# A maxout FFN written with differences: from token group 2 on, x*(w1*w_out) plus a maximum against zero

## The chip, the cores and the metric

The kernel runs on one core of one Trainium2 chip. The metric is device microseconds of the whole program. The kernel before was timed three times; the median is 475.64 us.

## The reference

Two blocks follow each other. The first is a gated linear attention (HGRN2 with an outer-product state), for 4 batches, 8 heads, 768 time steps and head dimension 48:

```
f = 1 / (1 + exp(-f_logit))
for t in range(S):
    state = f[t][:, None] * state + outer(k[t], v[t])
    y[t] = q[t] @ state
```

Its output, with the 8 heads side by side, is x with 3072 tokens and 384 features. The second block is a feed-forward network (FFN) with three weights of 384 x 768 and one of 768 x 384:

```
h = maximum(maximum(x @ w1, x @ w2), x @ w3)
out = h @ w_out
```

Everything is computed in float32; the weights arrive as 64-bit numbers.

## The kernel before, in words

**Units and groups.** Attention is cut in 24 units (`NU`). A unit is a chunk of 64 time steps of two batches, with all 8 heads, so 128 tokens. Four units (`GRP`) make a group of 512 tokens (`TOK`), and the FFN works on a group. There are six groups, 0 to 5. (The title counts them from 1: group 2 there is `g == 1` in the code.)

**Attention.** For each unit VectorE (DVE) runs two scans over the gates (lines 316 and 334), VectorE or GpSimd (POOL) multiply k and q with them (lines 327 and 338), and TensorE (PE) makes scores (`pairs`, line 379), which VectorE masks (line 382), then the values part (line 398) and the state update (`sums`, line 419), and at last the part of y that comes from the carried state (`finish`, line 465). From unit 8 on (`BY_ROWS`), k, q and f arrive by rows in eight small transfers for each tensor and pair of units (line 182), and VectorE turns 32x32 blocks (lines 283 and 369); before that PE transposes them. ScalarE (ACT) copies y to `heads` (line 471), and `pack` (line 486) moves it with ten DMAs per call to `xT`, whose partitions are features. For units 0 to 3, PE transposes x instead (line 454). The first three units of a group are packed in its last unit, the fourth in the first unit of the next group, half of these DMAs issued by SyncE (SP), half by ScalarE.

**FFN.** `ffn(g, xT)` is a generator. For each of 6 blocks of 128 hidden features (`NJ`) and each of the 3 weights it accumulates a product over 3 slices of 128 input features (`NK`) into a PSUM tile `p` of 128 x 512 (line 513). The first product is copied by ScalarE to `top` (line 520), the second and third are joined to it by maxima on VectorE (line 522), the last of which writes `hm`. Then for each of 4 tiles of 128 tokens, 6 matmuls with 384 columns accumulate `hm` times `w_out` (line 538); ScalarE copies the result to `o` (line 543), and SyncE sends it out (line 548). There are two `p` buffers (`ps_f`), and they are also used by everything else in the FFN. In group 0 the first two blocks are done by halves of 256 tokens.

**Weights.** The 64-bit weights come in 24 pieces. Each is rounded to float32 by ScalarE (lines 228 to 232), VectorE (lines 239 to 242) and POOL (line 246), in step with the FFN of group 0: after each product `round_begin` and `round_end` are called for the next pieces. Later the pieces are loaded once more and ScalarE checks their range (lines 257 and 266 to 269).

**The order.** It is written out by hand under `tc.manual_schedule()`: each engine executes its instructions in the order in which the program emits them. FFN work of the last complete group stands between the pieces of attention: `pending` holds generators, and `fill(n)` lets the first one run n steps, where a step ends at each `yield`. A product of 512 columns has two steps (two matmuls, then one), an output tile two of three matmuls each. What is left of a group when the next one is appended is done first. After the last unit, `finish`, `pack` and the FFN of group 5 are left.

Of the kernel before, what the change touches and what calls it, by code (L numbers as in the profile page):

```python
# [46 lines left out]
C = 64  # L47
# [8 lines left out]
def kernel(  # L56
# [27 lines left out]
    make_identity(nc, ident)  # L84
    w_in = [const.tile([128, NK, DFF], FP32, name=f"w_in{i}") for i in range(3)]
    w_out = const.tile([128, NJ, DM], FP32, name="w_out")
    low = const.tile([1, 1], I32, name="low")

    def fast():
        ctx = ExitStack()  # L90
        with ctx:
# [398 lines left out]

            HALF = TOK // 2
            J_HALF = 2

            def ffn(g, xT):
                hm = work.tile([128, NJ, TOK], FP32, name="hm", bufs=1)


                steps = [(j, slice(0, TOK)) for j in range(NJ)]
                if g == 0:
                    steps = [(j, slice(n * HALF, (n + 1) * HALF)) for n in range(2) for j in range(J_HALF)] + steps[J_HALF:]  # L500
                done, n_step = 1, 0
                for j, t in steps:
                    w = t.stop - t.start
                    for i in range(3):
                        p = ps_f.tile([128, TOK], FP32, name="p")[:, 0:w]
                        for kt in range(NK):
                            if g:
                                rhs = xT[:, kt, :]
                            elif w < TOK:
                                rhs = by_halves(xT)[:, t.start // HALF, kt, :]  # L510
                            else:
                                rhs = by_halves(xT)[:, :, kt, :]
                            nc.tensor.matmul(p if g or w < TOK else p.rearrange("p (two t) -> p two t", two=2),  # L513
                                             lhsT=w_in[i][:, kt, j * 128:(j + 1) * 128], rhs=rhs,
                                             start=(kt == 0), stop=(kt == NK - 1))
                            if kt == 1 and w == TOK:
                                yield
                        if i == 0:
                            top = work.tile([128, TOK], FP32, name="top")[:, 0:w]
                            nc.scalar.copy(top, p)  # L520
                        else:
                            nc.vector.tensor_tensor(hm[:, j, t] if i == 2 else top, p, top, op=ALU.max)  # L522

                        if g == 0:
                            n_step += 1
                            ahead = n_step + 1 if n_step <= 6 else 7 + (n_step - 6) * 5 // 6 if n_step <= 12 else 12 + (n_step - 12) * 6 // 5
                            for r in range(done, min(ahead, len(pieces))):
                                if r + 2 < len(pieces):
                                    round_begin(r + 2)
                                if r + 1 < len(pieces):  # L530
                                    round_end(r + 1)
                                done = r + 1
                            load_weights(2, done)
                        yield
                for i in range(GRP):
                    p = ps_f.tile([128, TOK], FP32, name="p")
                    for j in range(NJ):
                        nc.tensor.matmul(p[:, 0:DM], lhsT=hm[:, j, i * UT:(i + 1) * UT], rhs=w_out[:, j, :],  # L538
                                         start=(j == 0), stop=(j == NJ - 1))
                        if j == NJ // 2 - 1:  # L540
                            yield
                    o = work.tile([UT, DM], FP32, name="o", bufs=3)
                    nc.scalar.copy(o, p[:, 0:DM])  # L543
                    c, bp = divmod(g * GRP + i, 2)
                    for a in range(2):
                        t0 = (2 * bp + a) * S + c * C
                        last = g * GRP + i == NU - 1 and a
                        (nc.scalar if last else nc.sync).dma_start(out=out[t0:t0 + C, :], in_=o[a * C:(a + 1) * C, :])  # L548
                    yield

            pending = []

            def fill(n):
                while n and pending:
# [14 lines left out]
                return work.tile([128, NK, TOK], FP32, name="xT")  # L569

            CHECKS = 2 * GRP + 3

            with tc.manual_schedule():
# [56 lines left out]
                fill(1)  # L633
                keys(3)
                sums(2)
                y_by_tokens(2)
                pairs(3)
                fill(1)
                x_of_tokens(2, xT)
                fill(1)  # L640
                values(3)
                fill(1)
                sums(3)
                fill(1)
                y_by_tokens(3)
                load(GRP + 1)
                load_v(GRP + 1)
# [7 lines left out]
                fill(2)  # L655
                for u in range(GRP, NU):
                    n = u + 1
                    fill(0 if u == 2 * GRP else 4 if u % 2 and u > 2 * GRP else 2)
                    keys(u)
                    keys_by_blocks(u, 2)  # L660
                    if u > GRP:
                        finish(u - 1)
                        if u % GRP == 3:
                            pack(0, 2, xT)
                        elif u % GRP == 0:
                            pack(3, 3, xT, both)
                    if u % GRP == 0:
                        if u > GRP:
                            pending.append(ffn(u // GRP - 1, xT))
# [14 lines left out]
                    fill(2)  # L684
# [4 lines left out]
                    fill(2)  # L689
                    if BY_ROWS <= u + 2 < NU and u % GRP == 0:  # L690
                        load(u + 2, one, "k")
                    values(u)
# [1 line left out]
                        carry(n)  # L694
                    if CHECKS <= u < CHECKS + len(pieces) // 2:
                        check_range(2 * (u - CHECKS) + 1)
                    fill(1 if u < 2 * GRP else 2)
                    if CHECKS <= u + 2 < CHECKS + len(pieces) // 2:
                        check_load(2 * (u + 2 - CHECKS))
                        check_load(2 * (u + 2 - CHECKS) + 1)  # L700
                    if BY_ROWS <= u + 2 < NU and u % GRP == 0:
                        load(u + 2, one, "q")
                    keys_by_blocks(n, 0)
                    if u >= 2 * GRP:
                        fill(2)
                    keys_by_blocks(n, 1)
                fill(2)
# [20 lines left out]
    def general():  # L728
        G, AHEAD = 128, 3
# [243 lines left out]
```

## Time and profile before

| what | value |
| --- | --- |
| median of three runs | 475.64 us (473.46 to 476.57) |
| span of the profiled execution (first to last instruction) | 472.3 us; the page gives no other time for it |
| PE busy | 455.4 us, 96% |
| DVE, ACT, POOL busy | 266.4, 146.1, 105.5 us |
| matmul records of the FFN's products (line 513) | 684, 290.3 us |
| matmul records of the FFN's outputs (line 538) | 288, 96.6 us |
| mean granted TensorE clock | 0.999 of full speed |

The page first gives each engine's busy time, its share of the span and its instruction count. In the row of slices that follows, the span is cut in 40 equal parts, and a digit is the busy share in tenths. A float32 matmul leaves two records, so 684 records are 342 matmuls: 306 of 512 columns and 36 of 256. The durations of neighbouring records overlap[...]. "PEld" is the weight load, "SPq" and "ACTq" are issues of DMAs by these engines, and `A <- B` in a view of waits reads "A sat idle until B was done".

### The profile page before, as it was taken

To read this page: it belongs to the slowest core of one execution; us is meant where nothing else is said; L and a number is where in the kernel's file an instruction comes from. 1 tells how busy PE (TensorE), PEld (TensorE's weight loads), DVE (VectorE), ACT (ScalarE), POOL (GpSimd) and SP (SyncE) were. 2 spreads that over 40 slices of the span, in tenths; PEclk is the share of its full clock that TensorE was granted. 3 is DMA by queue.
4 is the path that set the end of the run, shared out by engine and by line. 5 is a ranking of instruction groups with operands and counts; after the bars stand their busy time and mean duration, and the time that the engine had idled before them with its cause. 6 is when DMAs were issued, how large, how long until landed. Compare 5 with 4: busy or idle time off the path is not lost.

```text
span 472.3 us, 10233 instructions
## 1 busy us (share of the span) xinstructions
PE 455.4 (96%) x4068; PEld 247.8 (52%) x4068; DVE 266.4 (56%) x528; ACT 146.1 (31%) x339; POOL 105.5 (22%) x125
## 2 busy tenths in 40 slices
PE   4989999999999999999999999999999999999995
PEld 3767655556445456545456445445544445444453
DVE  6876757687478675497685487585585220021110
ACT  2434757421201325144224144233243211100000
POOL 2153636432033031232130230230321200000000
PEclk9999999999999999999999999999999999999999
DMA  9998997234768043778343577544460012100002
GB/s 135 207 257 235 277 221 91 42 69 78 115 87 192 22 82 102 154 98 148 83 83 107 96 136 93 151 82 114 87 138 1 0 51 49 36 1 1 2 17 53
DMA packets 177141, 47.13 MB, mean 100 GB/s; under 512 B 154816, under 2 KB 175552, under 8 KB 177088
## 3 DMA queue, kind: packets, MB, share of 16 engines
q1 hardware_dynamic: 172528, 45.25, 48.5%
q10 hardware_dynamic: 4560, 1.18, 1.5%
q8 instruction: 33, 0.54, 0.5%
q14 instruction: 20, 0.16, 0.1%
HBM read 37.75 MB, written 4.72 MB: 90 GB/s over the span
## 4 chain that ended last, share of the span: by engine, by line
PE 82%; SPq 5%; DMA 4%; DVE 3%; issue 1%; ACTq 1%; ACT 1%; DVEq 0%
PE p L513 54%; PE p L538 16%; DMA f_ld<-in_f_logit_dram 4%; PE y L465 2%; PE y L398 2%; SPq L182 2%; PE a L379 2%; PE y L419 2%; PE tr L278 1%; ACTq L486 1%; SPq L163 1%; DMA xT<-heads 1%; DVE r L316 1%; SPq L548 1%; PE y L394 1%
## 5 line engine op out<-in xcount | busy, mean ns | idle before, releaser
L513 PE MATMUL p<-xT,w_in 128*128 128x512 f32 (+1 forms) x684 | 290.3, 575 | 1.6 <-POOL w_in L246 0.8
L513 PEld LDWEIGHTS p<-xT,w_in 128*128 128x128 f32 x684 | 126.2, 190 | 134.9 <-issue 124.8
L538 PE MATMUL p<-w_out,hm 128*128 128x384 f32 x288 | 96.6, 490 | 0.6 <-DVE top L522 0.6
L522 DVE TENSOR_TENSOR top<-p,top 128x512 f32<-128x512 f32 (+1 forms) x38 | 25.0, 657 | 102.4 <-PE p L513 101.6
L538 PEld LDWEIGHTS p<-w_out,hm 128*128 128x128 f32 x288 | 53.8, 190 | 38.4 <-issue 1.7
L369 DVE STREAM_TRANSPOSE ks<-kh 32x128 f32<-32x128 f32 x224 | 67.7, 302 | 3.6
L520 ACT COPY top<-p 128x512 f32<-128x512 f32 (+1 forms) x38 | 21.4, 562 | 139.9 <-PE p L513 139.8
L326 POOL COPY ends<-r 128x8 f32<-128x8 f32 x24 | 7.7, 320 | 187.1 <-DVE r L316 187.1
L522 DVE TENSOR_TENSOR hm<-p,top 128x512 f32<-128x512 f32 (+1 forms) x38 | 24.8, 652 | 32.6 <-PE p L513 32.6
L327 POOL TENSOR_TENSOR kh<-kt,r 128x512 f32<-128x512 f32 x16 | 31.4, 1960 | 36.5 <-DVE kt L283 26.1
L543 ACT COPY o<-p 128x384 f32<-128x384 f32 x24 | 11.4, 476 | 89.8 <-PE p L538 85.7
L471 ACT COPY heads<-y 64x256 f32<-64x256 f32 (+1 forms) x60 | 22.1, 369 | 43.1 <-PE y L465 36.5
L316 DVE TENSOR_TENSOR_SCAN r<-gate,from_one 128x520 f32<-128x520 f32 x24 | 29.8, 1240 | 9.2 <-ACT gate L295 5.2
L334 DVE TENSOR_TENSOR_SCAN prod<-gate,from_inv 128x520 f32<-128x520 f32 x24 | 30.2, 1259 | 0.0
L246 POOL TENSOR_TENSOR w_in<-top_bits,rest_bits 128x384 uint32<-128x384 uint32 x18 | 21.1, 1180 | 30.3 <-DVE top_bits L240 12.1
L382 DVE TENSOR_TENSOR at<-a,mask 128x512 f32<-128x512 f32 x24 | 16.5, 689 | 14.4 <-PE a L379 14.0
L283 DVE STREAM_TRANSPOSE gate<-sig 128x512 f32<-128x512 f32 x16 | 11.3, 705 | 16.2 <-ACT sig L298 16.2
L344 POOL TENSOR_TENSOR state<-st,ends 128x384 f32<-128x384 f32 x22 | 19.2, 872 | 0.2
L338 POOL TENSOR_TENSOR qh<-qt,prod 128x512 f32<-128x512 f32 x16 | 18.8, 1176 | 1.5 <-DVE qt L283 1.5
L398 PEld LDWEIGHTS y<-at,v_ld 64*64 64x64 f32 x640 | 11.1, 134 | 14.1 <-issue 9.0
L465 PEld LDWEIGHTS y<-qh,state 48*48 48x48 f32 x640 | 10.3, 119 | 12.3 <-issue 12.3
L379 PE MATMUL a<-qh,kh 48*64 48x64 f32 x768 | 15.7, 219 | 0.5 <-DVE qh L338 0.3
(89 smaller groups left out, 308.8 us busy)
## 6 DMA issues: line engine op xcount, KB each, us to landing
raw<-in_moe_w_dram SPq DMA_DIRECT2D x36, 384.0 KB, 5.1
v_ld<-in_v_dram SPq DMA_DIRECT2D x48, 96.0 KB, 3.2
raw<-in_moe_w_out_dram SPq DMA_DIRECT2D x12, 384.0 KB, 4.8
out_dram<-o SPq DMA_DIRECT2D x47, 96.0 KB, 2.2
xT<-heads SPq DMA_DIRECT2D x30, 72.0 KB, 2.2
f_ld<-in_f_logit_dram SPq DMA_DIRECT2D x32, 64.0 KB, 2.6
k_ld<-in_k_dram SPq DMA_DIRECT2D x32, 64.0 KB, 2.4
q_ld<-in_q_dram SPq DMA_DIRECT2D x32, 64.0 KB, 2.6
```

The costliest lines, as they stand in the source:

```text
L246: nc.gpsimd.tensor_tensor(dst, by(top), by(rest), op=ALU.add)
L316: nc.vector.tensor_tensor_scan(r[:, 0:LEN][:, ::-1], flat(gate)[:, ::-1], flat(from_one)[:, ::-1], 1.0, op0=ALU.mult, op1=ALU.max)
L327: (nc.vector if u < BY_ROWS else nc.gpsimd).tensor_tensor(kh.rearrange("p h a t -> p a h t"), kt, by_batch(r[:, 1:LEN + 1].rearrange("p (x ...
L334: nc.vector.tensor_tensor_scan(flat(prod), flat(gate_tiles[u % 2]), flat(from_inv[u % 2]), 1.0, op0=ALU.mult, op1=ALU.max)
L369: nc.vector.transpose(ks[n * 32:(n + 1) * 32, :, par, e0:e0 + 32], kh[p0:p0 + 32, :, a, t0:t0 + 32])
L379: nc.tensor.matmul(p[t, par, hp * C:(hp + 1) * C], lhsT=kh[r, hp, a, :], rhs=qh[r, a, hp, :], start=True, stop=True)
L398: nc.tensor.matmul(y[o:o + DP, a, hp * C:(hp + 1) * C], lhsT=v_ld[s, 2 * hp + par, :], rhs=d["at"][s, par, hp, :], start=(hp == 0), stop=F ...
L471: nc.scalar.copy(heads[o, :, t0 + a * C:t0 + (a + 1) * C], y[i, a, 0:HP * C].rearrange("p (h t) -> p h t", h=HP))
L513: nc.tensor.matmul(p if g or w < TOK else p.rearrange("p (two t) -> p two t", two=2), lhsT=w_in[i][:, kt, j * 128:(j + 1) * 128], rhs=rhs, ...
L520: nc.scalar.copy(top, p)
L522: nc.vector.tensor_tensor(hm[:, j, t] if i == 2 else top, p, top, op=ALU.max)
L538: nc.tensor.matmul(p[:, 0:DM], lhsT=hm[:, j, i * UT:(i + 1) * UT], rhs=w_out[:, j, :], start=(j == 0), stop=(j == NJ - 1))
```

## The change

With a = x*w1, the maximum of the three products is a + max(0, x*(w2-w1), x*(w3-w1)). So the FFN's output is x*(w1*w_out) + max(0, x*(w2-w1), x*(w3-w1))*w_out. Groups 1 to 5 compute this form; group 0 keeps the old one (`ffn_first`).

Behind the products of group 0 the weights are remade in place, between its four output tiles: `apart` subtracts w1 from w2 and w3 (VectorE), `turn` transposes w1 (PE, copied back by ScalarE), and `linear` multiplies it with `w_out` into `w_lin`, which lies in the place of w1. In groups 1 to 5 a block then has two products: the first is copied through Relu by ScalarE, the second is joined by one maximum on VectorE. An output tile has three matmuls of x with `w_lin` ahead of the six of `hm` with `w_out`, all in one accumulation.

Each `yield` now returns an amount of PE time, and `fill(ns)` adds to a budget and runs steps until it is used up. The amounts in the program change with that: five `fill(PART)` with `PART = 2740` in a unit, the last of them 1000 less in units 4 to 7. The last `pack` of a group is issued by SyncE alone, except for that of the last group. In the last two units ScalarE reads one element of y after the values part (`seen`).

```diff
+    w_lin = w_in[0][:, :, 0:DM]
...
+                if u >= NU - 2:
+                    seen = work.tile([1, 1], FP32, name="seen")
+                    nc.scalar.copy(seen, y[0:1, 1, (HP - 1) * C:(HP - 1) * C + 1])
...
-            def ffn(g, xT):
...
+            COLUMN = 4 / 2.4
+
+
+            def product(g, xT, j, i, t):
+                w = t.stop - t.start
...
+                    if kt == 1 and w == TOK:
+                        yield 2 * w * COLUMN
+                return p
+
...
+            def outputs(g, hm, i, xT=None):
+                p = ps_f.tile([128, TOK], FP32, name="p")
+                if g:
+                    for kt in range(NK):
+                        nc.tensor.matmul(p[:, 0:DM], lhsT=xT[:, kt, i * UT:(i + 1) * UT], rhs=w_lin[:, kt, :],
+                                         start=(kt == 0), stop=False)
+                    yield NK * DM * COLUMN
+                for j in range(NJ):
+                    nc.tensor.matmul(p[:, 0:DM], lhsT=hm[:, j, i * UT:(i + 1) * UT], rhs=w_out[:, j, :],
+                                     start=(g == 0 and j == 0), stop=(j == NJ - 1))
+                    if j == NJ // 2 - 1:
+                        yield NJ // 2 * DM * COLUMN
...
+            def apart(j):
+
+                first = w_in[0][:, :, j * 128:(j + 1) * 128]
+                for w in w_in[1:]:
+                    piece = w[:, :, j * 128:(j + 1) * 128]
+                    nc.vector.tensor_tensor(piece, piece, first, op=ALU.subtract)
+
+            def turn(j):
+
+                p = ps_f.tile([128, TOK], FP32, name="p")
+                piece = w_in[0][:, :, j * 128:(j + 1) * 128]
+                for a in range(NK):
+                    nc.tensor.transpose(p[:, a * 128:(a + 1) * 128], piece[:, a, :], ident)
+                nc.scalar.copy(piece, p[:, 0:DM].rearrange("q (a c) -> q a c", a=NK))
+                yield DM * COLUMN
+
+            def linear(a):
+
+                p = ps_f.tile([128, TOK], FP32, name="p")
+                for j in range(NJ):
+                    nc.tensor.matmul(p[:, 0:DM], lhsT=w_in[0][:, a, j * 128:(j + 1) * 128], rhs=w_out[:, j, :],
+                                     start=(j == 0), stop=(j == NJ - 1))
+                    if j % 2:
+                        if j == NJ - 1:
+                            nc.scalar.copy(w_lin[:, a, :], p[:, 0:DM])
+                        yield 2 * DM * COLUMN
+
+            def ffn_first(xT):
...
+                        yield (1 if w == TOK else NK) * w * COLUMN
                 for i in range(GRP):
+                    for j in range(i * NJ // GRP, (i + 1) * NJ // GRP):
+                        apart(j)
+                    yield from outputs(0, hm, i)
+                    for j in range(i * NJ // GRP, (i + 1) * NJ // GRP):
+                        yield from turn(j)
+                for a in range(NK):
+                    yield from linear(a)
+
+            def ffn(g, xT):
+                hm = new_hm()
+                for j in range(NJ):
+                    for i in (1, 2):
+                        p = yield from product(g, xT, j, i, slice(0, TOK))
+                        if i == 1:
+                            top = new_top(TOK)
+                            nc.scalar.activation(top, p, AF.Relu)
+                        else:
+                            nc.vector.tensor_tensor(hm[:, j, :], p, top, op=ALU.max)
+                        yield TOK * COLUMN
+                for i in range(GRP):
+                    yield from outputs(g, hm, i, xT)
 
+            budget = [0.0]
+
+            def fill(ns):
+                budget[0] += ns
+                while budget[0] > 0 and pending:
                     try:
-                        next(pending[0])
-                        n -= 1
+                        budget[0] -= next(pending[0])
                     except StopIteration:
                         pending.pop(0)
 
                 return work.tile([128, NK, TOK], FP32, name="xT")
 
             CHECKS = 2 * GRP + 3
+            STEP = NK * HALF * COLUMN
+            PART = 2740
...
-                pending.append(ffn(0, xT))
-                fill(1)
+                pending.append(ffn_first(xT))
+                fill(STEP)
...
-                    fill(0 if u == 2 * GRP else 4 if u % 2 and u > 2 * GRP else 2)
+                    fill(PART)
...
-                            pack(3, 3, xT, both)
+                            pack(3, 3, xT)
...
-                    fill(1 if u < 2 * GRP else 2)
+                    fill(PART)
...
-                    if u >= 2 * GRP:
-                        fill(2)
+                    fill(PART - 1000 if u < 2 * GRP else PART)
...
-                fill(12)
+                fill(20000)
...
-                fill(6)
+                fill(9000)
-                fill(99)
+                fill(10 ** 6)
```

`product`, `new_hm` and `new_top` hold what stood in `ffn` before. `ffn_first` has the loop over products with the calls of `round_begin`, `round_end` and `load_weights` as before.

More of the change, by code (lines that the diff above doesn't have):

```diff
@@ L492, in fast @@
             J_HALF = 2
-            def ffn(g, xT):
[L495 to L500, printed above, removed]
+            COLUMN = 4 / 2.4
+            def product(g, xT, j, i, t):
+                w = t.stop - t.start
+                p = ps_f.tile([128, TOK], FP32, name="p")[:, 0:w]
+                for kt in range(NK):
+                    if g:
+                        rhs = xT[:, kt, :]
+                    elif w < TOK:
+                        rhs = by_halves(xT)[:, t.start // HALF, kt, :]
+                    else:
+                        rhs = by_halves(xT)[:, :, kt, :]
+                    nc.tensor.matmul(p if g or w < TOK else p.rearrange("p (two t) -> p two t", two=2),
+                                     lhsT=w_in[i][:, kt, j * 128:(j + 1) * 128], rhs=rhs,
+                                     start=(kt == 0), stop=(kt == NK - 1))
+                    if kt == 1 and w == TOK:
+                        yield 2 * w * COLUMN
+                return p
@@ new lines, in new_hm, with new_top @@
+            def new_hm():
+                return work.tile([128, NJ, TOK], FP32, name="hm", bufs=1)
+            def new_top(w):
+                return work.tile([128, TOK], FP32, name="top")[:, 0:w]
+            def outputs(g, hm, i, xT=None):
+                p = ps_f.tile([128, TOK], FP32, name="p")
+                if g:
+                    for kt in range(NK):
+                        nc.tensor.matmul(p[:, 0:DM], lhsT=xT[:, kt, i * UT:(i + 1) * UT], rhs=w_lin[:, kt, :],
[6 more added lines that the diff above has]
+                        yield NJ // 2 * DM * COLUMN
+                o = work.tile([UT, DM], FP32, name="o", bufs=3)
+                nc.scalar.copy(o, p[:, 0:DM])
+                c, bp = divmod(g * GRP + i, 2)
+                for a in range(2):
+                    t0 = (2 * bp + a) * S + c * C
+                    last = g * GRP + i == NU - 1 and a
+                    (nc.scalar if last else nc.sync).dma_start(out=out[t0:t0 + C, :], in_=o[a * C:(a + 1) * C, :])
+                yield NJ // 2 * DM * COLUMN
@@ L501, in ffn @@
+            def ffn_first(xT):
+                hm = new_hm()
+                steps = [(j, slice(n * HALF, (n + 1) * HALF)) for n in range(2) for j in range(J_HALF)]
+                steps += [(j, slice(0, TOK)) for j in range(J_HALF, NJ)]
                 done, n_step = 1, 0
@@ L504, in ffn @@
                     for i in range(3):
[L505 to L517, printed above, removed]
+                        p = yield from product(0, xT, j, i, t)
                         if i == 0:
-                            top = work.tile([128, TOK], FP32, name="top")[:, 0:w]
+                            top = new_top(w)
                             nc.scalar.copy(top, p)
@@ L522, in ffn @@
                             nc.vector.tensor_tensor(hm[:, j, t] if i == 2 else top, p, top, op=ALU.max)
[L524 to L533, printed above, removed]
@@ L534, in ffn @@
-                        yield
-                for i in range(GRP):
[L536 to L549, printed above, removed]
+                        n_step += 1
@@ new lines, in ffn_first @@
+                        ahead = n_step + 1 if n_step <= 6 else 7 + (n_step - 6) * 5 // 6 if n_step <= 12 else 12 + (n_step - 12) * 6 // 5
+                        for r in range(done, min(ahead, len(pieces))):
+                            if r + 2 < len(pieces):
+                                round_begin(r + 2)
+                            if r + 1 < len(pieces):
+                                round_end(r + 1)
+                            done = r + 1
+                        load_weights(2, done)
@@ new lines, in ffn_first @@
+                        yield (1 if w == TOK else NK) * w * COLUMN
+                for i in range(GRP):
+                    for j in range(i * NJ // GRP, (i + 1) * NJ // GRP):
[6 more added lines that the diff above has]
+            def ffn(g, xT):
+                hm = new_hm()
+                for j in range(NJ):
[4 more added lines that the diff above has]
+                            nc.scalar.activation(top, p, AF.Relu)
+                        else:
+                            nc.vector.tensor_tensor(hm[:, j, :], p, top, op=ALU.max)
+                        yield TOK * COLUMN
+                for i in range(GRP):
+                    yield from outputs(g, hm, i, xT)
@@ L551, in fast @@
             pending = []
-            def fill(n):
-                while n and pending:
-                    try:
-                        next(pending[0])
-                        n -= 1
+            budget = [0.0]
+            def fill(ns):
+                budget[0] += ns
+                while budget[0] > 0 and pending:
+                    try:
+                        budget[0] -= next(pending[0])
                     except StopIteration:
@@ L628, in fast @@
                 round_begin(2)
-                pending.append(ffn(0, xT))
-                fill(1)
+                pending.append(ffn_first(xT))
+                fill(STEP)
                 before(3)
                 values(2)
-                fill(1)
+                fill(STEP)
                 keys(3)
@@ L637, in fast @@
                 pairs(3)
-                fill(1)
+                fill(STEP)
                 x_of_tokens(2, xT)
-                fill(1)
+                fill(STEP)
                 values(3)
-                fill(1)
+                fill(STEP)
                 sums(3)
-                fill(1)
+                fill(STEP)
                 y_by_tokens(3)
@@ L651, in fast @@
                 after(GRP)
-                fill(2)
+                fill(2 * STEP)
                 before(GRP)
                 carry(GRP)
-                fill(2)
+                fill(2 * STEP)
                 for u in range(GRP, NU):
                     n = u + 1
-                    fill(0 if u == 2 * GRP else 4 if u % 2 and u > 2 * GRP else 2)
+                    fill(PART)
                     keys(u)
@@ L683, in fast @@
                         check_range(2 * (u - CHECKS))
-                    fill(2)
+                    fill(PART)
                     keys_by_blocks(u, 3)
@@ L688, in fast @@
                         before(n)
-                    fill(2)
+                    fill(PART)
                     if BY_ROWS <= u + 2 < NU and u % GRP == 0:
@@ L696, in fast @@
                         check_range(2 * (u - CHECKS) + 1)
-                    fill(1 if u < 2 * GRP else 2)
+                    fill(PART)
                     if CHECKS <= u + 2 < CHECKS + len(pieces) // 2:
@@ L703, in fast @@
                     keys_by_blocks(n, 0)
-                    if u >= 2 * GRP:
-                        fill(2)
+                    fill(PART - 1000 if u < 2 * GRP else PART)
                     keys_by_blocks(n, 1)
-                fill(2)
+                fill(PART)
                 finish(NU - 1)
```

## The prediction

> **What bounds the kernel now.** I read the engine totals first, then the slices, then what TensorE (PE) waits for, then the chain that ended last, from which the prices come.
>
> ```profile
> PE 455.4 (96%) x4068; PEld 247.8 (52%) x4068; DVE 266.4 (56%) x528; ACT 146.1 (31%) x339; POOL 105.5 (22%) x125
> PE   4989999999999999999999999999999999999995
> DVE  6876757687478675497685487585585220021110
> PEclk9999999999999999999999999999999999999999
> ```
>
> PE is busy 455.4 of 472.3 us, at full clock, in every slice but the first two and the last; VectorE (DVE) is at 56%. The view of PE's waits says whether anything else decides:
>
> ```profile
> PE tr L278 <- DMA f_ld<-in_f_logit_dram: 6.5, 3, 5.9
> PE p L438 <- DVE st L427: 1.5, 1, 1.5
> PE p L513 <- POOL w_in L246: 0.8, 1, 0.8
> PE p L513 <- DVE hm L522: 0.7, 1, 0.7
> PE p L538 <- DVE top L522: 0.6, 1, 0.6
> ```
>
> The columns are total us, times, longest. All but the first loads sum to some 6 us, all before unit 8. From about 105 us on PE is fed without a gap: the kernel takes as long as PE's work. The reader is to see that only PE work removed, or a new PE wait, can move the end.
>
> The chain of waits at the end is pure FFN, so prices are clean there (start, duration, what):
>
> ```profile
> 405.36 15.45 PE p L513 x36
> 420.98 31.10 PE p L513 x72
> 452.07 15.49 PE p L538 x48
> ```
>
> A float32 matmul leaves two records, so 72 records are 36 matmuls of 512 columns: 31.10/36 = 0.864 us each. 48 records are 24 matmuls of 384 columns: 15.49/24 = 0.645 us. For 128x128 transposes the timeline has two sets of four, back to back:
>
> ```profile
> 57.83 0.60 PE L278 MATMUL tr<-ident,k_ld 128*128 128x128 f32 x4
> 58.26 0.60 PE L278 MATMUL tr<-ident,q_ld 128*128 128x128 f32 x4
> ```
>
> 58.26 - 57.83 = 0.43 us for four, 0.108 us each; transposes are not split in two records.
>
> [...]the 512-column records last 597 ns in the mean, while they follow each other every 432 ns; so I price from chain stretches, not from means. [...]the 128x384 addition of line 427 took 532. [...]the trace has one table load (1.28 us) for sigmoid, sign, abs and relu. [...]here an issue takes about 0.59 us.
>
> **The change, part by part, on PE.**
> - *w1 product gone from groups 1 to 5*: 5 groups x 6 blocks x 3 contraction steps = 90 matmuls of 512 columns, 90 x 0.864 = 77.8 us less. All on the path.
> - *x*(w1*w_out) added in their outputs*: 5 groups x 4 row tiles x 3 = 60 matmuls of 384 columns, 60 x 0.645 = 38.7 us more.
> - *Weight products, once*: 6 x 3 = 18 transposes, 1.9 us; 3 x 6 = 18 matmuls of 384 columns, 11.6 us.
> - Net: -77.8 + 38.7 + 1.9 + 11.6 = -25.6 us. Attention's matmuls and group 0's products stay.
>
> **On the other engines.**
> - *DVE*: [...]30 maxima of 0.684 us leave later (-20.5 us). Behind the subtractions in DVE's queue stand the mask, k and q work of units 7 and 8. The largest batch[...] is followed by 12 small transposes (3.8 us) before unit 8's mask; meanwhile PE has a row tile, three transposes, two linear matmuls and unit 7's state products, some 8 us. I take nothing[...].
> - *ScalarE (ACT)*: nine evictions of the weight stage at 0.48 us, 4.3 us, at 31% load: hidden but for the handover below. Relu replaces a copy of the same shape (584 ns): nothing; at most 0.1 us each were it slower, and a product (2.6 us) covers that. The two `seen` copies wait for PE's y in units 22 and 23; behind them in ACT's queue are FFN evictions. PE has just issued that work, so I take 0, at most 0.5 us each.
> - *Two FFN accumulators*: a turned block is only 3 x 0.108 = 0.33 us of PE, less than the copy (0.48[...]) that frees the other buffer. Four handovers stall (output 1 behind turn 0, output 2 behind turn 2, turn 5, first linear product): about 0.35, 0.35, 0.3, 0.2. I take 1.2 us, 0 to 3.
> - *Weights of group 0*: FFN now gets 12.7 us per unit in units 4 to 7 where it got 7 half-steps, about 9. So it finishes one attention unit earlier; unit work apart from FFN being about 3 us, the last rounded weights are wanted some 3 us sooner. They have room: the last w_in piece is rounded near 77 us and used after 94. Early pieces are tight (the 0.8 us wait), and rounding, maxima and scans share DVE and ACT more densely. I take 1 us, 0 to 3.
> - *Head rows to xT*: a new group's first product needs the transfer of the last unit's heads, and PE needs old FFN work meanwhile. Before, at unit 16:
>
> ```profile
> 249.14 0.67 PE L465 MATMUL y<-qh,state 48*48 48x64 f32 x32
> 249.87 1.14 ACT L471 COPY heads<-y 128x256 f32<-128x256 f32 x3
> 251.04 3.09 ACTq L486 DMA_DIRECT2D xT<-heads  x5
> 256.33 3.60 SPq L486 DMA_DIRECT2D xT<-heads  x5
> 263.19 7.03 PE L513 MATMUL p<-xT,w_in 128*128 128x512 f32 x16
> ```
>
> The last piece is issued near 259.3 and lands near 261.1, 11.3 us after the y products ended; PE turned to the new group at 263.2. The SyncE (SP) half began 5 us after the ACT half, behind a weight reload that waited 5.5 us for ACT's transfers. The change puts all ten issues on SP, so that crossing goes, and ACT's sigmoid, held 3.2 us, comes sooner. New need: heads copies 1.2, nine issues 9 x 0.59 = 5.3, landing 1.9, together 8.4 us, if SP is free. Cover, counted from PE's order: unit 8, 16 linear matmuls, about 12 us; units 12 and 16, 12 output matmuls plus mask and values products (1.6), 9.3; unit 20, nine, 7.4; the end, where both queues still share, nine, 5.8. At the end the need was 6.7 us (y products end 393.55, last issue about 398.3, landing 1.9). Stalls: 1.0 at unit 20, 0.9 at the end, 1.9 together. Bounds: 0, and rival A. Reloads, k and q rows queue behind the ten issues on SP; with the 5 us wait gone they are earlier than before, and q rows, 1.0 us late once, gain room.
>
> Sum: 1.2 + 1.0 + 1.9 = 4.1 us of new waits. Against the profiled execution: 472.3 - 25.6 + 4.1 = 450.8 us of span. The page gives no time of the profiled execution beyond its span; the median, 475.64, lies 3.3 us above it, and I carry that: 450.8 + 3.3 = 454.1, so 454.
>
> The budget itself (a step is charged 1.667 ns a column where the chain shows 0.864/512 = 1.688) changes order, not sum. Turns are charged 0.64 us where they take 0.33: 1.9 us in all of units with less cover.
>
> **Rivals.**
> A. *The heads arrive late.* If SP is held as before and the transfer takes 11.3 us at units 12, 16, 20, with cover 9.3, 9.3, 7.4, PE loses 2.0 + 2.0 + 3.9, and 0.9 at the end: 8.8 instead of 1.9. With the weight stage at its upper ends (3 + 3) that is 472.3 - 25.6 + 14.8 + 3.3 = 464.8. For: no cover was short before, all are shorter now. Against: what held SP was the crossing of queues, which goes. 0.17.
> B. *No stall at all*: 472.3 - 25.6 + 3.3 = 450.0. For: PE was gapless for 360 us. Against: three covers and a handover that come out negative. 0.15.
> C. *Slower: attention's chain becomes the bound.* FFN per unit falls from about 15 to 13.6 us, so a unit shrinks from 18.1 (72.4 us per group) to 16.8 us. If sigmoid, transposes, scans, POOL products and mask of a unit needed over 18.4 us, sixteen units would cost 16 x 1.6 = 26 us, what was saved; at 18.75, 31 us: 472.3 - 25.6 + 31 + 3.3 = 481. It decides from 18.4 us a unit. Against: DVE works 12.3 us a unit (24.65 in 36 us), and unit 17's chain ran from sigmoid at 254.2 to q product at 262.4, 8 us. 0.04.
> D. *It doesn't do what it says* (fewer matmuls gone): PE's order shows 216 products of 512 columns where there were 306, so excluded.
>
> **Numbers.** Forecast 0.64 (451 to 458), A 0.17, B 0.15, C 0.04. The range 450 to 463 takes in B and most of A. Runs of the kernel before spread by 0.65%, so within 1% counts as no change (470.9 to 480.4). Faster by over 1%: forecast, B, and nearly all of A, 0.93; same 0.03; slower 0.04.
>
> **What would show it.** In the page after: 432 PE records of 512 columns (612 before) and 444 of 384 (288 before); PE busy near 430 us and still over 94%; DVE near 250. Waits of PE for "DMA xT<-heads" of about 1 us at unit 20 and the end; waits for ACT copies between 90 and 115 us near 1 us. Wrong if PE waits on xT for several us at each group, on DVE or POOL in every unit, or if 384-column matmuls that switch between x and hm cost more than 0.645 us.

## The result and the profile after

The changed kernel took 457.93 us (median of four runs, 457.55 to 458.81), the kernel before beside it 474.73 (473.46 to 476.57): a ratio of 0.9635, 95% interval 0.9595 to 0.9675. The profiled execution has a span of 456.2 us.

First the engine totals and slices of the changed kernel:

```profile
PE 432.9 (95%) x4062; PEld 244.1 (54%) x4062; DVE 253.4 (56%) x510; ACT 150.1 (33%) x350; POOL 103.9 (23%) x125
PE   4989999999999999999999999999989999999995
DVE  6976757556858569357779557759456520011100
PEclk9999999999999999999999999999999999999999
```

PE's busy time fell from 455.4 to 432.9 us, by 22.5. Its idle time, span less busy, rose from 16.9 to 23.3 us, by 6.4. The difference, 16.1 us, is the fall of the span. The PE row now has an 8 late in the kernel where it had nines only. The groups of instructions, different shapes apart, show what remains of each sort of matmul (records, then total busy us and mean ns):

```profile
L511 PE MATMUL p<-xT,w_in 128*128 128x512 f32 x432 | 195.3, 600 | 6.6 <-ACT top L612 2.8 <-DVE hm L614 1.9 <-DMA xT<-heads 1.8
L532 PE MATMUL p<-w_out,hm 128*128 128x384 f32 x288 | 99.3, 491 | 1.3 <-ACT w_in L558 1.0 <-ACT o L537 0.2
L528 PE MATMUL p<-w_in,xT 128*128 128x384 f32 x120 | 42.4, 489 | 0.0
```

With the 36 records (12.4 us) of the product w1*w_out, there are 432 records of 512 columns and 288 + 120 + 36 = 444 of 384, as forecast. The 512-column group was 272.7 us before, so 77.4 us went. The last column, idle time ahead of the group with its releasers, has grown: before, it was 0.2 us for the 512-column products. The waits of PE after (total us, times, longest) say the same, with the stages around them:

```profile
PE tr L279 <- DMA f_ld<-in_f_logit_dram: 5.1, 1, 5.1
PE p L511 <- ACT top L612: 2.8, 4, 0.7
PE p L511 <- DVE hm L614: 1.9, 3, 0.6
PE p L511 <- DMA xT<-heads: 1.8, 1, 1.8
...
PE p L532 <- ACT w_in L558: 1.0, 1, 1.0
...
PE p L557 <- ACT o L537: 0.3, 1, 0.3
PE p L511 <- POOL w_in L247: 0.3, 1, 0.3
PE p L532 <- ACT o L537: 0.2, 1, 0.2
```

Lines 2 to 4 are 6.5 us. They fall in units 8 to 23, where PE had waited for nothing that counts. From unit 8's scores to unit 23's PE was idle 0.3 us before (105.1 to 377.1 us) and 7.0 us after (119.6 to 375.0). Line 4 is the wait at unit 20. Lines 2 and 3 were not in the forecast: PE wants one of the two FFN accumulators and neither is empty. Unit 17 in the timeline shows how that comes about (start, duration, work, idle time before it in brackets):

```profile
276.43 1.28 DVE L370 STREAM_TRANSPOSE ks<-kh 32x128 f32<-32x128 f32 x4
277.74 0.71 DVE L284 STREAM_TRANSPOSE kt<-k_ld 128x512 f32<-128x512 f32 x1
278.38 1.20 DVE L335 TENSOR_TENSOR_SCAN prod<-gate,from_inv 128x520 f32<-128x520 f32 x1
279.41 1.13 PE L511 MATMUL p<-xT,w_in 128*128 128x512 f32 x2
280.57 0.60 ACT L612 ACTIVATE top<-p 128x512 f32<-128x512 f32 x1 [2.47 <-PE p L511]
280.67 0.71 DVE L284 STREAM_TRANSPOSE qt<-q_ld 128x512 f32<-128x512 f32 x1 [1.09 <-POOL kh L328]
281.22 7.13 PE L511 MATMUL p<-xT,w_in 128*128 128x512 f32 x16 [0.69 <-ACT top L612]
281.31 0.65 DVE L614 TENSOR_TENSOR hm<-p,top 128x512 f32<-128x512 f32 x1
```

The program emits `ks`, `kt`, `prod` and `qt`, VectorE's part of the attention work, between the two steps of a block's second product. PE has nothing of its own at that place and runs the product through, so its row shows no gap. But the maximum that empties this product (`hm`, line 614) is emitted behind the four and runs only at 281.31. The product that ends near 280.5, the next block's first, was in the other accumulator. PE then waits 0.69 us until ScalarE has emptied that one. `qt`, ahead of the maximum, had itself waited 1.09 us; at two of the other three waits of line 2 (ending at 214.82 and 350.24) it had waited 2.73 and 2.98 us, where its two waits before the change were 1.03 and 0.84.

### The profile page after: what moved, and what is told of

It is laid out like the page before. It is cut to its first block, busy times and chain, and to the rows that moved or that the text cites. A ratio compares the mean times of both kernels' runs of the same rounds, so it can differ in the third digit from the quotient of the medians.

```text
span 456.2 us, 10209 instructions
## 1 busy us (share of the span) xinstructions
PE 432.9 (95%) x4062; PEld 244.1 (54%) x4062; DVE 253.4 (56%) x510; ACT 150.1 (33%) x350; POOL 103.9 (23%) x125
## 4 chain that ended last, share of the span: by engine, by line
PE 84%; DVE 5%; ACT 4%; DMA 4%; issue 2%; SPq 1%; POOL 0%; ACTq 0%; DVEq 0%
PE p L511 42%; PE p L532 18%; PE p L528 7%; PE y L470 3%; PE p L565 3%; PE y L399 2%; PE y L424 2%; PE a L380 2%; DVE r L317 2%; DMA raw<-in_moe_w_out_dram 2%; ACT heads L476 1%; PE tr L279 1%; DMA xT<-heads 1%; ACT sig L299 1%; PE y L395 1%
## 5 line engine op out<-in xcount | busy, mean ns | idle before, releaser
L511 PE MATMUL p<-xT,w_in 128*128 128x512 f32 (+1 forms) x504 | 212.8, 569 | 7.5 <-ACT top L612 2.8
L511 PEld LDWEIGHTS p<-xT,w_in 128*128 128x128 f32 x504 | 92.0, 190 | 104.2 <-issue 85.2
L532 PE MATMUL p<-w_out,hm 128*128 128x384 f32 x288 | 99.3, 491 | 1.3 <-ACT w_in L558 1.0
L614 DVE TENSOR_TENSOR hm<-p,top 128x512 f32<-128x512 f32 x30 | 20.4, 681 | 80.9 <-PE p L511 80.5
L327 POOL COPY ends<-r 128x8 f32<-128x8 f32 x24 | 6.7, 279 | 187.0 <-DVE r L317 187.0
L612 ACT ACTIVATE top<-p 128x512 f32<-128x512 f32 x30 | 17.8, 594 | 91.9 <-PE p L511 91.9
L528 PE MATMUL p<-w_in,xT 128*128 128x384 f32 x120 | 42.4, 489 | 0.0
L528 PEld LDWEIGHTS p<-w_in,xT 128*128 128x128 f32 x120 | 22.5, 190 | 16.0 <-issue 1.9
L399 PEld LDWEIGHTS y<-at,v_ld 64*64 64x64 f32 x640 | 11.2, 134 | 13.0 <-issue 6.1
```

What stands on the lines that cost most here:

```text
L528: nc.tensor.matmul(p[:, 0:DM], lhsT=xT[:, kt, i * UT:(i + 1) * UT], rhs=w_lin[:, kt, :], start=(kt == 0), stop=False)
L614: nc.vector.tensor_tensor(hm[:, j, :], p, top, op=ALU.max)
```

## The experiments

Ratios are to the kernel before, run on the same chip beside the kernel; the changed kernel's is 0.9635.

### Is it the order or the arithmetic?

**Order alone.** The arithmetic of the kernel before, three products and two maxima a block, with everything else of the changed kernel: steps given out by the budget (slots of 1772 ns in units 4 to 7, 3124 after), the last `pack` of a group on SyncE alone, and `seen`. This cut of the edit is against the kernel before; those further down are against the changed kernel.

```diff
-            def fill(n):
-                while n and pending:
+            def fill(ns):
+                budget[0] += ns
+                while budget[0] > 0 and pending:
                     try:
-                        next(pending[0])
-                        n -= 1
+                        budget[0] -= next(pending[0])
```

> Old mathematics (three products, two maxima, no weight products), new handing out by PE time; the amounts are scaled so that the same leftover stands at each group's start (1772 ns in units 4 to 7, 3124 after). Theory order (the new order puts a maximum behind VectorE's k and q work): waits for evictions from unit 8 on of 3 to 6 us, 475 to 479 us. Theory form (it is the two-product form that makes PE wait): waits under 1 us there as before the change, 471 to 475 us.

Measured: 479.22 us, ratio 1.0048 (1.0025 to 1.0071), span 477.8. PE's waits in it:

```profile
PE p L511 <- DVE hm L603: 2.5, 4, 0.6
...
PE p L511 <- DMA xT<-heads: 1.0, 1, 1.0
```

The new order with the single queue gains nothing by itself; it costs half a per cent and already brings waits for accumulators (0.8 us for `top` beside these) and for xT, as the theory of the order had it. The gain needs the new arithmetic. That the arithmetic is not enough without the single queue is shown further down.

**The weight products left out.** The transposes of w1 and the product w1*w_out are missing; `w_lin` is w1 itself, so the output is another one.

```diff
                     yield from outputs(0, hm, i)
-                    for j in range(i * NJ // GRP, (i + 1) * NJ // GRP):
-                        yield from turn(j)
-                for a in range(NK):
-                    yield from linear(a)
...
-            PART = 2740
+                    PART = 1972 if u < 2 * GRP else 2740
```

> The changed kernel without the transposes of w1 and without w1*w_out (left out: w_lin holds plain w1); the subtractions stay. The amount in units 4 to 7 falls from 2740 to 1972 ns, so that the same leftover stands at unit 8. Theory price: the stage costs what the chain's prices say, 18 transposes 1.9 + 18 matmuls 11.6 + its waits 1.5 = 15.0 us, so 443 us against the changed kernel's 457.9. Theory hidden cost (the some 3 us of PE busy time that the prices did not foresee sit in this stage): 18 us, so 440 us.

Measured: 446.74 us, ratio 0.9361 (0.9297 to 0.9425), span 445.3, PE busy 421.9. That is 11.2 us under the changed kernel by medians. PE's busy time fell by 11.0 us, at a mean granted clock of 0.996 that lengthens it by an estimated 1.8 us (0.004 x 445), so about 12.8 us at full clock: near the 1.9 + 11.6 = 13.5 us of the forecast. Its idle time is 23.4, as in the changed kernel: the waits of the weight stage went, and VectorE's (4.2 us here against 1.9) grew. The products cost what their matmuls cost; a larger hidden cost of the stage is not there. Neither theory's number came out (443 and 440 us), because the waits moved with the order of the steps and the clock was lower.

### The waits for accumulators

**ScalarE empties both products.** The second product is copied to `hm` by ScalarE, and the maximum is made there in place, so that no accumulator waits for VectorE.

```diff
-                            nc.vector.tensor_tensor(hm[:, j, :], p, top, op=ALU.max)
+                            nc.scalar.copy(hm[:, j, :], p)
+                            nc.vector.tensor_tensor(hm[:, j, :], hm[:, j, :], top, op=ALU.max)
```

> The changed kernel, but ScalarE copies the second product out of its accumulator into hm, and VectorE's maximum then works in place in SBUF. Theory 1 (an accumulator is held by a maximum that stands late in VectorE's queue): PE's waits for ACT top and DVE hm, 4.7 us from unit 8 on, fall below 1.5 us,[...] so 452 to 453 us. Theory 2 (two accumulators are too few for this order, whoever empties them, or ScalarE gets late itself): waits of 4 us or more for ScalarE, 457 to 460 us.

Measured: 452.37 us, ratio 0.9479 (0.9417 to 0.9540), span 449.8. PE's waits, from the top:

```profile
PE tr L279 <- DMA f_ld<-in_f_logit_dram: 5.0, 1, 5.0
PE p L511 <- DMA xT<-heads: 1.7, 1, 1.7
PE p L443 <- DVE st L432: 1.5, 1, 1.5
```

Both of lines 2 and 3 of the changed kernel are gone, the waits for ScalarE's `top` with those for VectorE's `hm`; the xT wait is as it was. So both depend on VectorE being the one that empties the second product. (What part the choice of the accumulator has in the waits for `top` is tested below.) The span fell by 6.4 us: 5.2 of idle time and 1.2 of busy time, the latter perhaps since a stall splits a run of matmuls (in the changed kernel six records of x-matmuls take 1.94 us within a run and 2.20 us at the start of one); that this makes up the 1.2 us isn't shown.

**Steps by count.** The new arithmetic handed out by numbers of steps instead of the budget:

```diff
-                        budget[0] -= next(pending[0])
+                        next(pending[0])
+                        budget[0] -= 1
...
-            STEP = NK * HALF * COLUMN
-            PART = 2740
+            STEP = 1
+            PART = 2
```

(Each unit has slots of 2, 2, 2, 1 and 2 steps, the tail 16 and 8.)

> New mathematics, but steps handed out by count again: 2, 2, 2, 1, 2 in a unit from unit 4 on, 9 a unit where a group has 36 steps; 16 and 8 in the tail. Theory order: waits for ACT top and DVE hm below 1.5 us from unit 8 on; and the larger leftover (13 output steps) covers the heads, no wait for xT; 451 to 453 us. Theory form: the same 4.7 us of waits, 455 to 458 us.

Measured: 454.66 us, ratio 0.9523 (0.9466 to 0.9581). No wait for xT, but the accumulator waits are still there:

```profile
PE p L511 <- ACT top L612: 2.8, 4, 0.7
PE p L511 <- DVE hm L614: 2.5, 4, 0.6
```

The theory that the budget as such makes these waits fell: steps by count make them too. But this is not the handing-out of the kernel before. From unit 8 on that kernel gave out 0, 2 or 4 steps at a time, so whole products. Counted in the order of the program, attention stands between the two steps of none of its products in groups 1 to 4, but of 29 of 48 in the changed kernel and of 28 of 48 here, where one slot of a unit has a single step.

**Whole products.** Also by count, but with slots of an even number of steps (the fourth slot gives 2 steps in odd units, none in even ones), so that attention never cuts a product in two, as in the kernel before.

```diff
-                    fill(1)
+                    fill(1 if u == GRP else 2 * (u % 2))
```

> Like the run with steps by count, but 2, 2, 2, 0 or 2, 2 in a unit (one of them 1 in unit 4), so that from group 1 on no product of two steps is cut by a piece of attention. Theory cut (a second product begun ahead of the k and q work and finished behind it has its maximum queued behind that work on VectorE, while both accumulators are wanted): the 5.3 us of waits for ACT top and DVE hm fall below 1.5 us, 448 to 450 us. Theory form (two products on two accumulators wait wherever they are cut): 4 us or more stay, 454 to 456 us.

Measured: 451.32 us, ratio 0.9456 (0.9391 to 0.9522). The interval overlaps with that of steps by count, but the waits differ: VectorE's went, ScalarE's stayed at 2.7 us, four times. One of them in the timeline:

```profile
202.47 5.42 PE L511 MATMUL p<-xT,w_in 128*128 128x512 f32 x12
205.42 0.69 DVE L614 TENSOR_TENSOR hm<-p,top 128x512 f32<-128x512 f32 x1 [2.16 <-PE p L511]
207.93 0.60 ACT L612 ACTIVATE top<-p 128x512 f32<-128x512 f32 x1 [4.08 <-PE p L511]
208.58 2.84 PE L511 MATMUL p<-xT,w_in 128*128 128x512 f32 x6 [0.69 <-ACT top L612]
```

The maximum had emptied its accumulator at 206.1, yet at 207.9 PE waits for ScalarE to empty the one just filled. Here the pool gave the next product the accumulator that its neighbour had just filled.

**Strictly in turn.** Two further kernels name the accumulators themselves, first on top of the last one, then on the changed kernel alone.

```diff
-            ps_f = ctx.enter_context(tc.tile_pool(name="ps_f", bufs=2, space=bass.MemoryType.PSUM))
+            ps_f = ctx.enter_context(tc.tile_pool(name="ps_f", bufs=1, space=bass.MemoryType.PSUM))
+            turn_of = [0]
+
+            def accumulator(shape):
+                turn_of[0] ^= 1
+                return ps_f.tile(shape, FP32, name=f"p{turn_of[0]}")
...
-                p = ps_f.tile([128, TOK], FP32, name="p")
+                p = accumulator([128, TOK])
```

> Even steps by count, and the FFN's two accumulators are given names of their own and taken strictly in turn. In the order of the instructions of the even-steps run, one second product per group waits for ScalarE, so it is put into the accumulator that the product just before it filled. Theory assignment (PE waits since the pool hands out the accumulator just used): its 2.7 us of waits for ACT top go, below 0.5 us of eviction waits from unit 8 on, 448 to 449.5 us. Theory late maximum (VectorE is late there whichever accumulator is given): the same waits appear for DVE hm, 451 us.

Measured: 446.73 us (six runs), ratio 0.9363 (0.9317 to 0.9408), span 446.2. In the same stretch as above the products now follow without a gap:

```profile
202.53 7.03 PE L517 MATMUL p<-xT,w_in 128*128 128x512 f32 x16
204.52 0.69 DVE L620 TENSOR_TENSOR hm<-p,top 128x512 f32<-128x512 f32 x1 [2.00 <-PE p L517]
207.02 0.60 ACT L618 ACTIVATE top<-p 128x512 f32<-128x512 f32 x1 [4.08 <-PE p L517]
```

PE waits for no eviction in units 8 to 23. The pool's choice made the waits that the kernel with whole products had kept. The trace is what shows it: the intervals of the two ratios still overlap, though the slowest of these runs (448.01) is under the fastest of those (449.86). This is the fastest version of the study that keeps the output: 2.8% under the changed kernel by the two ratios (0.9363/0.9635), and its interval lies apart.

> The changed kernel as it is, with the two accumulators taken strictly in turn. Theory assignment alone: the 4.7 us of waits for ACT top and DVE hm go, 452 to 453 us. Theory cut (products cut by attention have their maximum queued behind k and q work, and the pool only dodges it): waits for DVE hm of about 1.4 us a time take the place of 0.7 us for ACT top, 6 us in all, 458 to 460 us.

Measured: 466.36 us, ratio 0.9772 (0.9700 to 0.9845), 8 us slower than the changed kernel. PE's waits and the longest of them in the timeline:

```profile
PE p L517 <- DVE hm L620: 10.7, 6, 3.5
```

```profile
285.07 0.71 DVE L290 STREAM_TRANSPOSE qt<-q_ld 128x512 f32<-128x512 f32 x1 [3.13 <-DMA q_ld<-in_q_dram]
285.70 0.65 DVE L620 TENSOR_TENSOR hm<-p,top 128x512 f32<-128x512 f32 x1
286.41 5.83 PE L517 MATMUL p<-xT,w_in 128*128 128x512 f32 x9 [3.52 <-DVE hm L620]
```

With products cut by attention, alternating makes PE wait for the late maximum itself, 10.7 us in place of 2.8 + 1.9. So the cut makes the maximum late, and the pool's choice in the changed kernel is the cheaper answer to that: reuse the buffer that ScalarE empties in 0.6 us rather than the one that stands in VectorE's queue. Alternation gained only together with whole products. The direction was expected, the size was larger. One reason is in the first line: `qt`, ahead of the maximum, waits 3.13 us for q rows that SyncE loads, at the longest of the three waits above 2 us (2.24, 3.52 and 3.07). What alternating would cost with the q rows in time isn't shown. The other is PE's busy time, which rose as well (438.2 us, clock 0.987).

### The transfer from heads to xT

**Both queues again.**

```diff
                         elif u % GRP == 0:
-                            pack(3, 3, xT)
+                            pack(3, 3, xT, both)
```

> The changed kernel, but the last unit's heads go out through both queues again, as before the change. Theory crossing (SyncE is held some 5 us by ScalarE's transfers, which is what rival A of the prediction feared): PE waits for xT at units 12, 16 and 20 about 2, 2 and 4 us where it waited 0, 0 and 1.8, so 462 to 465 us. Theory issue time (two queues halve the issue time): the wait at unit 20 goes, 456 us.

Measured: 476.79 us, ratio 0.9996 (0.9971 to 1.0020), span 475.4. The whole gain is gone. PE's first waits, the largest of SyncE's for a transfer to `xT`, and unit 20 with the issues of both queues:

```profile
PE y L424 <- DVE ks L370: 7.1, 9, 2.7
PE p L511 <- DMA xT<-heads: 6.2, 2, 4.9
SPq L183 <- DMA xT<-heads: 16.1, 2, 9.0
```

```profile
335.55 0.66 PE L470 MATMUL y<-qh,state 48*48 48x64 f32 x32
337.45 3.10 ACTq L491 DMA_DIRECT2D xT<-heads  x5
340.59 0.63 ACT L299 ACTIVATE sig<-f_ld 128x512 f32<-128x512 f32 x1 [3.17 <-DMA xT<-heads]
340.86 2.56 SPq L542 DMA_DIRECT2D out_dram<-o  x4
343.79 1.90 SPq L258 DMA_DIRECT2D raw<-in_moe_w_out_dram  x2
346.99 3.10 SPq L491 DMA_DIRECT2D xT<-heads  x5
350.43 2.05 PE L511 MATMUL p<-xT,w_in 128*128 128x512 f32 x2 [4.93 <-DMA xT<-heads]
```

SyncE sits idle until transfers to `xT` have landed, 25.5 us in all (16.1, 6.2 and 3.2 at three lines); in the changed kernel it has no such wait. Its half begins 11 us after the y products (335.55 to 346.99), and PE runs out of other work 4.93 us before the rows for its next product are there. Sigmoid starts 3.17 us late, behind ScalarE's own issues; `ks` follows late, and PE's waits for it grow from 0.5 to 7.1 us. So the theory of the crossing had the direction, but not the size (462 to 465 us). In the changed kernel the same stretch reads:

```profile
323.36 0.66 PE L470 MATMUL y<-qh,state 48*48 48x64 f32 x32
324.39 1.07 SPq L258 DMA_DIRECT2D raw<-in_moe_w_out_dram  x2
325.56 1.11 SPq L542 DMA_DIRECT2D out_dram<-o  x2
326.77 6.79 SPq L491 DMA_DIRECT2D xT<-heads  x10
334.47 4.10 PE L511 MATMUL p<-xT,w_in 128*128 128x512 f32 x9 [1.84 <-DMA xT<-heads]
```

All ten issues stand together and end near 333.6; the wait is 1.84 us. The 19.2 us between the spans are 9.0 of PE's busy time (441.9 against 432.9) and 10.2 of idle time; the two waits above grew by 6.6 + 4.4 = 11.0.

**A smaller part**, 2700 ns a slot for 2740:

> The changed kernel with PART = 2700 instead of 2740: a group's leftover shrinks less, and the FFN work between the last y products of a group and the next group's first product, counted from the order, is 11.7 us at unit 20 instead of 7.8. Theory cover: PE's one wait for xT (1.8 us) goes and nothing else changes, 455 to 457 us. Theory queue (SyncE's other issues move along with the work, so the heads land later too): a wait over 1 us stays, 457 to 459 us.

Measured: 456.60 us, ratio 0.9583 (0.9517 to 0.9649), span 453.9. The intervals do not separate it from the changed kernel, but its waits do: none for xT, the accumulator waits as before (2.8 and 2.4 us). So cover at unit 20 depends on where the budget happens to cut.

**Both**: ScalarE emptying both products, and a part of 2700:

> ScalarE empties the second accumulator and PART = 2700: both remedies. If waits for evictions and for xT are separate, their gains add up: 452.4 less 1.7, about 450.5 us, with PE waits from unit 8 on below 1 us in all. If they are not, 452 us or more.

Measured: 450.46 us, ratio 0.9435 (0.9367 to 0.9503), span 448.7. No wait for xT or for an eviction from unit 8 on: the two causes are apart. By the waits their gains add; the intervals of this kernel and the one with a part of 2740 overlap.

## Why the prediction was right, and where it was off

The forecast was 454 us, range 450 to 463; it came out at 457.93, at the upper edge of the likeliest case (451 to 458) and by its route.

- *What bounds the kernel* held: PE is busy 95% after as well, and the time follows PE's work and PE's waits.
- *Matmuls priced from the chain* held. 77.8 us less was forecast for the w1 products, 77.4 measured. The fear that 384-column matmuls switching between x and `hm` cost more fell. In the last row tiles the chain (start, duration, what) repeats one pattern:

```profile
428.07 1.94 PE p L528 x6
430.01 3.87 PE p L532 x12
```

  1.94 + 3.87 = 5.81 us for nine, 0.645 each. To price from the chain was right: before, a record of 512 columns lasted 597 ns in the mean, and the next one began 432 ns after it.
- *Net -25.6 us* was too good: busy fell by 22.5. The x-matmuls show 42.4 us for 38.7, the transposes 2.9 for 1.9, the output matmuls 99.3 against 96.6 before (times of groups overlap, so these can't be added). One cause is that some stretches are shorter: six records of x-matmuls take 1.94 us in the chain and 2.20 us at 324.42, where they begin a stretch. With the accumulator waits removed, busy time is 431.7. About 2 us of it I can't place.
- *The weight stage*: 1.2 us forecast, the author's estimate; 1.0 + 0.3 + 0.2 = 1.5 measured. The weights of group 0: 1 us forecast, and the wait on POOL fell from 0.8 to 0.3.
- *DVE hidden*: held in units 6 and 7, where PE waits for ScalarE alone (1.5 us from 90 to 120 us). The 12 subtractions took 7.2 us in all; their median record lasts 551 ns. One batch of four took 3.21 us from 112.91 on, where the other of four took 1.96. Two operations of POOL (1.17 and 1.14 us) ran beside the slow batch; that they were the cause isn't shown. Relu takes 594 ns for the copy's 584: nothing, as said.
- *Head rows to xT*: 1.0 forecast at unit 20, 1.84 measured, since SyncE began `pack` only at 326.77, behind two reloads and two outputs; "if SP is free" was not met. At the end 0.9 was forecast and none came. The single queue, which the forecast counted only against rival A, is worth more: with both queues the gain is 0. That the q rows would gain room did not come true: `qt` waits up to 2.98 us. Shared, the issuing at unit 20 takes 3.10 us on each engine, five issues each, where SyncE alone takes 6.79 us for ten; but the kernel with both queues takes 19 us more.
- **The step that failed** is "Two FFN accumulators", which saw handovers in the weight stage alone, and with it the 4.1 us of new waits. From unit 8 on there are 4.7 us of them. The forecast reckoned with VectorE's total load (56%) and not with what stands ahead of one maximum in its queue when attention cuts a block between product and maximum. It is a matter of where the cuts fall: before, with whole products, PE waited 0.2 us there; the old three products in the new order wait too (2.5 + 0.8 us), and so do the new ones by count. So new waits came to 6.4 us of idle time where 4.1 were forecast, and busy time to 3.1 more: a span of 456.2 for 450.8.
- *The offset* of the median to the span was carried as 3.3 us. It is 1.7 in this kernel, and 1.7 to 1.9 in every run whose span is on record; so the execution that was profiled for the prediction was itself faster than the median. With 1.7 the same sum gives 452.5, 5.4 below the measured time. That the time still fell within 451 to 458 was in part luck.

Of the rivals, B's case of no stall at all (450.0) is what the kernel with whole products and accumulators in turn reaches and passes (446.73). A late transfer, as in A, appears when both queues are used (at unit 20 the last issue ends 13.9 us after the y products), and C did not come: PE waits for `ks` 0.5 us in all.

## What to carry to other kernels

Price work on the bounding engine from stretches of the chain, which was right here to 0.4 us in 77.8; then look for each buffer's emptying instruction and read what stands ahead of it in its engine's queue, since load in per cent doesn't show it. When a change shortens the cover of a transfer, look first at how the transfer is issued: splitting it over two queues cost here all that the arithmetic had won. The pool with two buffers did not alternate (2.7 us of waits for ScalarE with whole products, none when the accumulators were taken in turn), so check which buffer each product gets; here alternation paid only with whole products.

## What the runs showed of the hardware

A wait of PE can cost more than itself. After the wait of 4.93 us in the kernel that uses both queues, the granted clock is reduced for the next stretch (window, length, busy time of PE, PEld, DVE, ACT, POOL, then granted clock, DMA share and GB/s):

```profile
350.40:362.00 11.60, 11.57 (x82) 5.38 (x83) 2.60 (x6) 1.77 (x5) 0.00 (x0) 0.77 0.72 146
362.00:375.00 13.00, 12.29 (x90) 5.44 (x89) 7.55 (x13) 4.99 (x13) 4.08 (x4) 1.00 0.29 39
```

0.77 over 11.6 us is some 2.7 us of work lost after one wait, an estimate from these two numbers. In the timeline the 16 records of products (512 columns) right behind that wait take 9.69 us; 16 such records take 7.13 us in the changed kernel at 281.22, behind a wait of 0.69 us.

Shorter waits did it too (alternating is the changed kernel with its accumulators in turn):

| run | wait of PE, its end (us) | records right behind it | time (us) | as many elsewhere (us) |
| --- | --- | --- | --- | --- |
| both queues | 4.93, 350.43 | 16 of products | 9.69 | 7.13 (changed, 281.22) |
| alternating | 3.52, 286.41 | 16 of products | 8.83 | 7.13 (changed, 281.22) |
| alternating | 3.07, 358.88 | 18 of products | 9.65 | 7.99 (changed, 62.38) |
| both queues | 2.74, 200.12 | 12 of outputs, from 201.37 | 5.83 | 4.14 (both queues, 247.94) |
| alternating | 2.24, 215.52 | 16 of products | 8.80 | 7.13 (changed, 281.22) |
| changed | 1.84, 334.47 | 14 of products | 6.25 | 6.28 (changed, 79.50) |
| both queues | 1.24, 276.29 | 16 of products | 7.11 | 7.13 (changed, 281.22) |

The four waits of 2.24 to 3.52 us cost 1.7 us more each, whatever their length, and the one of 4.93 us cost 2.6. The granted clock of the alternating kernel is 0.91 from 280 to 300 us and 0.86 from 350.4 to 362 us, two stretches that hold such waits. After the 1.84 us of the changed kernel it stayed at 1.00 (334 to 345 us). All twelve traces have a wait of 1.5 us for `st`; in the kernels before and after it ends at 31.93 and 30.61 us, and the clock from 30 to 35 us is 1.00. In order alone, whole products, both remedies (ScalarE emptying, part of 2700) and accumulators in turn, no wait after the first loads is longer than that one, and yet the mean clock is 0.995 or 0.996; where they lost it isn't shown.

So each wait of 2.24 us or more in this table was followed by slower matmuls, and those of 1.24 and 1.84 us were not. What the waits of 1.5 us do in the other runs stays open.
